# Shorter runs of empty matmuls in the opening of a fused RWKV-5 attention and squared-ReLU FFN kernel

## The chip, the cores and the metric

The kernel runs on one core of a Trainium2 chip. The metric is the device time of one execution in microseconds; lower is better. Engines are named as in the profile: PE is TensorE, PEld its weight loads, DVE VectorE, ACT ScalarE, POOL GpSimd, SP SyncE; SPq and POOLq are the parts of SP and POOL that issue transfers.

## The reference

The attention runs over r, k and v of shape (4, 8, 768, 48): batch, heads, tokens, head width. For each batch and head it keeps a 48 x 48 state:

```
y[t]  = r[t] @ (state + outer(u * k[t], v[t]))
state = w[:, None] * state + outer(k[t], v[t])
```

The eight heads of a token are put side by side (8 x 48 = 384), which gives x with 3072 rows, and the FFN follows:

```
h = maximum(x @ w_in, 0)          # 384 x 2048
out = (h * h) @ w_out             # 2048 x 384
```

All inputs and the output are float32.

## The kernel before, in words

The 768 tokens of each batch are cut into six chunks of 128, so there are 24 units (chunk, batch); units 0 to 3 are the first chunk of the four batches. A unit goes through these steps, and each step is one short function of the class `Do`:

- `ld` brings r, k or v of the unit to the chip (SP issues it, line 388). `kh` and `rh` scale k and r by powers of w into the bf16 tile rk (lines 428, 434).
- `T` transposes rk on PE with eight matmuls against an identity (line 464), and `Tc` copies the result from its PSUM bank to the tile rkT on ACT (line 286). Later units use a transposing transfer, `XB`, instead.
- `A` multiplies the transposed k and r (line 494), `Bm` masks the product on DVE (line 507), `Y` multiplies it with v in bf16 (`vb`) and, from unit 4 on, adds the state's part (lines 531, 527). `P0`, `P1`, `du` and `dv` make the part with u; `xs` adds it to Y on DVE (line 560).
- `U`, `S0`, `ts` and `S` carry the state to the next chunk.
- `X` transposes the unit's result on PE (line 578), and `xTc` copies it to the FFN's input xT; later units use a transfer, `xX`.

The FFN works on groups of units: the first two groups are one unit each, the other eleven are two. `F1.g.s` makes one slice of h for group g (line 594), `re` and `sq` take the maximum with zero and the square on ACT or DVE (lines 602, 604, 609, 613), `F2.i.f.n` adds n of the 16 parts of the second product for unit i (line 622), `os` and `out` bring the result to memory.

The weights w_in come as slices of 384 KB into staging tiles `st` (`lW.0.s`, issued by SP, line 399) and are cast to bf16 by `cW.0.s` on ACT, DVE or POOL (lines 286, 288). For groups of one unit F1.g.s uses the cast slices 2s and 2s + 1: F1.0.2 needs cW.0.4 and cW.0.5, F1.1.3 needs cW.0.6 and cW.0.7. Slice 2 and all of w_out come by a casting transfer that POOL issues (`W`, line 418).

The order of all steps is written out by hand in the string `ORDER` (line 24). A step is written as name, unit or group, then a colon, the engine (A, D, G for POOL, P, S for SP) and the buffer slots that it uses. The loop at line 676 issues the steps in that order, so each engine runs its own steps strictly in the order of the string and waits only for data and for slots. PE's first steps are

```
Z.83.6  T.3  T.0  Z.31.6  A.0  A.3  T.1  Z.22.0  A.1  T.2  U.0  Y.0  Z.15.7  X.0  A.2  Z.8.0 ...
```

`Z.n.b` is a run of empty matmuls: identity times identity into the PSUM bank b, which nobody reads before it is overwritten. n counts units of 128 columns; n // 4 of the matmuls are wide (128 x 512, line 648), and the n % 4 that remain are narrow (128 x 128, line 650). They wait for nothing but the identity. All of them stand in the opening, before the last PE step of F1.0.2.

Of the kernel before, what the change touches and what calls it, by code (L numbers as in the profile page):

```python
# [22 lines left out]
POOLS = dict(ldr=7, ldk=7, ldv=7, st=6, rk=7, P0=5, dv=5, vb=8, rkT=7, Bm=6, xs=5, hr=6, hq=30, os=4, ts=2, xT1=2, xT2=3)  # L23
ORDER = """
ld.r.0:S/0 ld.k.3:S/0 w:A shw:D u:S shu:D tab:A logw:A WkQ:A/0 kh.3:D/0 ld.k.0:S/1 P0.0:G/0 WtQ:A/1 rh.0:D/1 ld.r.3:S/1
rh.3:D/0 Z.83.6:P T.3:P/2 Tc.3:A/0 kh.0:D/1 ld.r.1:S/2 rh.1:D/2 P0.3:G/1 P1.3:G ld.r.2:S/3 rh.2:D/3 du.3:D/0 ld.k.2:S/2
T.0:P/3 Tc.0:A/1 Z.31.6:P A.0:P/4/5 ld.k.1:S/3 A.3:P/6/7 kh.2:D/3 kh.1:D/2 T.1:P/2 P1.0:G du.0:D/1 Tc.1:A/2 lW.0.0:S/0
P0.1:G/2 Bm.0.0:D/0 Bm.0.1:D/1 Bm.3.1:D/2 ld.v.0:S/0 Z.22.0:P A.1:P/1/3 P1.1:G du.1:D/2 T.2:P/0 cW.0.0:A vb.0:G/0 U.0:P/2
Bm.1.0:D/3 lW.0.1:S/1 dv.0:G Y.0:P/4 xs.0:D/0 cW.0.1:A Z.15.7:P X.0:P/5 ld.v.3:S/1 vb.3:G/1 dv.3:G Bm.1.1:D/4 Bm.3.0:D/5
Tc.2:A/3 A.2:P/7/1 Bm.2.1:D/0 ld.v.1:S/2 dv.1:G ld.v.2:S/3 vb.2:G/2 Z.8.0:P Y.3:P/4 vb.1:A/3 xs.3:D/1 Y.1:P/3 U.3:P/6  # L30
xs.1:D/2 xTc.0:A/0 F1.0.0:P/0 X.3:P/1 xTc.3:A/0 lW.0.4:S/2 cW.0.4:A WtS:A U.2:P/4 X.1:P/3 Bm.2.0:D/1 lW.0.5:S/3 Y.2:P/5
P0.2:G/3 xTc.1:D/1 F1.1.0:P/1 re.1.0:A/0 lW.0.6:S/4 cW.0.6:A P1.2:G re.0.0:D/1 du.2:D/3 dv.2:D cW.0.5:G Z.7.3:P F1.0.2:P/7
W.0.2:G F1.1.2:P/3 re.1.2:A/2 lW.0.7:S/5 cW.0.7:D F1.1.3:P/1 re.1.3:A/3 xs.2:D/3 X.2:P/0 xTc.2:D/0 F1.0.3:P/3 re.0.3:A/4
re.0.2:D/5 sq.0.2:D2/0 sq.1.3:D2/1 lW.0.3:S/0 cW.0.3:G W.1.0:G W.1.1:G ld.r.4:S/4 rh.4:D/4 WkS:A wc:S F1.2.4:P/1 WLcol:A
WLm:G F1.2.1:P/5 re.2.1:D/5 sq.2.1:D2/2 re.2.4:A/3 sq.2.4:A0/3 sq.1.0:A0/4 F1.2.3:P/0 re.2.3:A/5 ld.k.4:S/4 P0.4:D/4 kh.4:G/4
# [78 lines left out]
    kh=["rk{0}"], rh=["rk{0}"], T=["bT{0}"], Tc=["rkT{0}"], XB=["rkT{0}"], A=["bA{0}0", "bA{0}1"], Bm=["Bm{0}{1}"], Y=["bY{0}"],  # L114
    xs=["xs{0}"], U=["bU{0}"], ts=["ts{0}"], X=["bX{0}"], xTc=["xT{0}"], xX=["xT{0}"], F1=["bH{0},{1}"], re=["hr{0},{1}"],
# [608 lines left out]
```

## Time and profile before

| | |
|---|---|
| three timed runs | 176.63, 174.48, 176.38 us (median 176.38) |
| the profiled execution | 175.66 us, span 173.5 us |
| PE busy | 163.4 us, 94% of the span, 1718 matmuls |
| DVE, ACT, POOL busy | 138.6, 105.8, 100.3 us |
| transfers | 29.13 MB; q1 (SP's and ACT's) 73.8% of 16 engines' span, q0 (POOL's) 6.2% |
| wide empty matmuls (line 648) | 38, busy 10.9 us, first start at 2.7 us, last at 20.1 us |
| narrow empty matmuls (line 650) | 14 |

The profile describes one execution. All its times count from the start of the span, so 8.80 is 8.80 us after it. Matmuls are pipelined: the starts of the weight loads show the pace of PE better than the lengths of the matmuls. An entry such as `[0.40 <-DMA ldk<-in_k_dram]` says that the engine was idle for 0.40 us just before, until that transfer landed. The chain that ended last follows the end of the execution back, at each step to what released it.

### The profile page before, as it was taken

The page shows a single profiled execution, that of the slowest core. Times are in us where ns is not written, and L with a number is a line of the kernel's source. Part 1 is how long each engine was busy: PE and PEld are TensorE (multiplying, and loading weights), DVE is VectorE, ACT ScalarE, POOL GpSimd, SP SyncE. Part 2 cuts the span into 40 slices and gives each one's busy share as a digit, 9 for nine tenths or more (in the row PEclk, how much of TensorE's full clock was granted, in tenths as well). Part 3 has the DMA queues.
Part 4 walks back from the last instruction along what each step waited for, and adds up shares of the span by engine and source line. Part 5 has one row for each costly group of instructions (what it writes and reads, how often), then busy time and mean ns, then how long its engine had stood idle before and what let it go on. Part 6 is the DMA issues. An engine that isn't in the chain of part 4 may idle for free.

```text
span 173.5 us, 4403 instructions
## 1 busy us (share of the span) xinstructions
PE 163.4 (94%) x1718; PEld 121.8 (70%) x1718; DVE 138.6 (80%) x257; ACT 105.8 (61%) x189; POOL 100.3 (58%) x118
## 2 busy tenths in 40 slices
PE   3999989989999999999997999899999999998992
PEld 1476869756877777877775786686786886875871
DVE  5789879979997798989798999799979776970430
ACT  2359669764787395777564894475693482451940
POOL 5678957525199999877959763788635805100000
PEclk9999999999999999999999999999999999999999
DMA  4999999999998989999799893994991451321202
GB/s 96 229 278 225 326 217 178 213 215 191 214 196 163 225 195 210 177 194 279 148 223 204 167 227 97 191 213 84 193 229 44 106 128 37 126 68 29 91 3 88
DMA packets 105588, 29.13 MB, mean 168 GB/s; under 512 B 98008, under 2 KB 105568, under 8 KB 105568
## 3 DMA queue, kind: packets, MB, share of 16 engines
q1 hardware_dynamic: 103672, 26.95, 73.8%
q0 software_dynamic: 1744, 1.77, 6.2%
q8 instruction: 13, 0.21, 0.5%
q10 hardware_dynamic: 152, 0.14, 0.2%
q14 instruction: 7, 0.06, 0.1%
HBM read 20.46 MB, written 4.72 MB: 145 GB/s over the span
## 4 chain that ended last, share of the span: by engine, by line
PE 57%; DMA 13%; DVE 8%; SPq 8%; POOL 6%; issue 3%; ACT 2%; DVEq 0%; POOLq 0%
PE bank L594 25%; PE bank L622 23%; SPq L388 6%; DMA xT<-xs 5%; DMA st<-in_moe_w_in_dram 4%; DMA rkT<-rk 3%; DVE hq L613 2%; PE bank L494 2%; SPq L399 2%; DMA ldv<-in_v_dram 2%; PE bank L531 2%; PE bank L636 2%; PE bank L527 1%; ACT hr L602 1%; ACT hq L609 1%
## 5 line engine op out<-in xcount | busy, mean ns | idle before, releaser
L594 PE MATMUL bank<-xT,W 128*128 128x256 bf16 (+1 forms) x624 | 71.0, 264 | 2.0 <-DMA xT<-xs 1.3
L622 PE MATMUL bank<-W,hq 128*128 128x384 bf16 x368 | 68.4, 326 | 0.2 <-ACT hq L609 0.2
L594 PEld LDWEIGHTS <-W 128*128 128x128 bf16 x624 | 55.7, 98 | 11.4 <-DMA xT<-xs 1.0
L602 ACT ACTIVATE hr<-bank 128x512 bf16<-128x512 f32 x65 | 38.1, 592 | 24.6 <-PE bank L594 22.5
L609 ACT ACTIVATE hq<-hr 128x512 bf16<-128x512 bf16 x71 | 43.3, 627 | 13.5 <-DVE hr L604 12.3
L622 PEld LDWEIGHTS <-hq 128*128 128x128 bf16 x368 | 34.2, 98 | 18.8 <-ACT hq L609 0.6
L507 DVE TENSOR_TENSOR Bm<-bank,maskJT 128x512 bf16<-128x512 f32 x48 | 31.3, 681 | 3.7 <-PE bank L494 3.7
L604 DVE TENSOR_SCALAR hr<-bank 128x512 bf16<-128x512 f32 x31 | 21.1, 685 | 10.4 <-PE bank L594 10.1
L449 POOL TENSOR_TENSOR dv<-ldv,du 128x384 f32<-128x384 f32 x18 | 16.4, 913 | 14.2 <-DVE du L444 9.4
L441 POOL TENSOR_TENSOR P<-P,ub 128x384 f32<-128x384 f32 x18 | 18.9, 1055 | 7.0 <-DVE P L437 6.4
L437 POOL TENSOR_TENSOR P<-ldr,ldk 128x384 f32<-128x384 f32 x16 | 16.6, 1042 | 3.4 <-DMA ldk<-in_k_dram 3.4
L560 DVE TENSOR_TENSOR xs<-bank,dv 128x384 bf16<-128x384 f32 x24 | 13.1, 553 | 4.5 <-PE bank L531 2.7
L573 POOL TENSOR_TENSOR S0W<-ts,WLm 128x384 bf16<-128x384 f32 x11 | 11.1, 1017 | 9.5 <-DVE ts L570 9.3
L428 POOL TENSOR_TENSOR rk<-ldk,Wkhat 128x384 bf16<-128x384 f32 x14 | 15.3, 1097 | 2.2 <-DMA ldk<-in_k_dram 2.1
L286 ACT COPY os<-bank 128x384 f32<-128x384 f32 (+1 forms) x17 | 7.9, 462 | 13.4 <-PE bank L622 11.5
L444 DVE TENSOR_REDUCE du<-P 128x8 f32<-128x384 f32 x24 | 13.0, 546 | 0.9 <-POOL P L441 0.7
L648 PE MATMUL bank<-identity 128*128 128x512 bf16 x38 | 10.9, 431 | 2.7 <-POOL identity masks.py:199 2.7
L613 DVE TENSOR_TENSOR hq<-hr 128x512 bf16<-128x512 bf16 x25 | 11.9, 488 | 0.3
L434 POOL TENSOR_TENSOR rk<-ldr,Wt 128x384 bf16<-128x384 f32 x9 | 9.9, 1102 | 2.1 <-DMA ldr<-in_r_dram 2.1
L531 PE MATMUL bank<-vb,Bm 128*128 128x48 bf16 x192 | 10.9, 183 | 0.2 <-DVE Bm L507 0.2
L286 ACT COPY rkT<-bank 128x1024 bf16<-128x1024 bf16 x7 | 7.0, 1014 | 6.5 <-PE bank L464 6.5
L531 PEld LDWEIGHTS <-Bm 128*128 128x128 bf16 x192 | 9.3, 96 | 1.3 <-DVE Bm L507 0.7
(67 smaller groups left out, 160.2 us busy)
## 6 DMA issues: line engine op xcount, KB each, us to landing
ldr<-in_r_dram SPq DMA_DIRECT2D x24, 192.0 KB, 3.7
ldk<-in_k_dram SPq DMA_DIRECT2D x24, 192.0 KB, 3.8
ldv<-in_v_dram SPq DMA_DIRECT2D x24, 192.0 KB, 4.4
out_dram<-os SPq DMA_DIRECT2D x23, 192.0 KB, 3.0
st<-in_moe_w_in_dram SPq DMA_DIRECT2D x7, 384.0 KB, 5.3
W<-in_moe_w_out_dram POOLq DMA_DIRECT2D x4, 384.0 KB, 7.0
rkT<-rk SPq DMA_TRANSPOSE x17, 3.7
W<-in_moe_w_in_dram POOLq DMA_DIRECT2D x1, 192.0 KB, 5.0
```

The costliest lines, as they stand in the source:

```text
L428: e.tensor_mul(scaled("k", i), loaded("k", i), early("WkQ") if i < EARLY else Wkhat)
L437: e.tensor_mul(P0b[slot[f"P{i}"]], loaded("r", i), loaded("k", i))
L441: e.tensor_mul(t, t, ub)
L449: e.tensor_mul(dvb[slot[f"dv{i}"]], loaded("v", i), t)
L507: e.tensor_mul(o, a, mask_b)
L531: e.matmul(y[:, hc, D * h : D * (h + 1)], m[h][:, hc, :], vb[:, 2 * hc + h, :], start=(i < B), stop=True, skip_group_check=True,)
L594: e.matmul(hp[:, fi, :], W1[f // 2][:, c, 128 * (f % 2) : 128 * (f % 2 + 1)], xt[:, c, :], start=(c == 0), stop=(c == CCH - 1), skip_group ...
L602: e.activation(hr, hp, AF.Relu)
L604: e.tensor_scalar_max(hr, hp, 0.0)
L609: e.activation(hq, hr, AF.Square)
L613: e.tensor_mul(hq, hr, hr)
L622: e.matmul(bank(f"bO{i}")[:, 0:d_model], hqb[slot[f"hq{g},{f // m}"]][:, at : at + L], W2[f // 4][:, f % 4, :], start=(summed[i] == 1), st ...
```

## The change

Four of the six runs of empty matmuls get a smaller count. Nothing else differs: the steps, their order and their slots are those of before.

```diff
-rh.3:D/0 Z.83.6:P T.3:P/2 Tc.3:A/0 ...
+rh.3:D/0 Z.48.6:P T.3:P/2 Tc.3:A/0 ...
-T.0:P/3 Tc.0:A/1 Z.31.6:P A.0:P/4/5 ...
+T.0:P/3 Tc.0:A/1 Z.30.6:P A.0:P/4/5 ...
-Bm.1.0:D/3 lW.0.1:S/1 dv.0:G Y.0:P/4 xs.0:D/0 cW.0.1:A Z.15.7:P X.0:P/5 ...
+Bm.1.0:D/3 lW.0.1:S/1 dv.0:G Y.0:P/4 xs.0:D/0 cW.0.1:A Z.14.7:P X.0:P/5 ...
-P0.2:G/3 xTc.1:D/1 F1.1.0:P/1 ... cW.0.5:G Z.7.3:P F1.0.2:P/7
+P0.2:G/3 xTc.1:D/1 F1.1.0:P/1 ... cW.0.5:G Z.6.3:P F1.0.2:P/7
```

| run | before: wide + narrow | after: wide + narrow |
|---|---|---|
| first, ahead of T.3 | 20 + 3 | 12 + 0 |
| second, ahead of A.0 | 7 + 3 | 7 + 2 |
| third, Z.22, ahead of A.1 | 5 + 2 | 5 + 2 |
| fourth, ahead of X.0 | 3 + 3 | 3 + 2 |
| fifth, Z.8, ahead of Y.3 | 2 + 0 | 2 + 0 |
| sixth, ahead of F1.0.2 | 1 + 3 | 1 + 2 |

More of the change, by code (lines that the diff above doesn't have):

```diff
@@ L25 @@
 ld.r.0:S/0 ld.k.3:S/0 w:A shw:D u:S shu:D tab:A logw:A WkQ:A/0 kh.3:D/0 ld.k.0:S/1 P0.0:G/0 WtQ:A/1 rh.0:D/1 ld.r.3:S/1
-rh.3:D/0 Z.83.6:P T.3:P/2 Tc.3:A/0 kh.0:D/1 ld.r.1:S/2 rh.1:D/2 P0.3:G/1 P1.3:G ld.r.2:S/3 rh.2:D/3 du.3:D/0 ld.k.2:S/2
-T.0:P/3 Tc.0:A/1 Z.31.6:P A.0:P/4/5 ld.k.1:S/3 A.3:P/6/7 kh.2:D/3 kh.1:D/2 T.1:P/2 P1.0:G du.0:D/1 Tc.1:A/2 lW.0.0:S/0
+rh.3:D/0 Z.48.6:P T.3:P/2 Tc.3:A/0 kh.0:D/1 ld.r.1:S/2 rh.1:D/2 P0.3:G/1 P1.3:G ld.r.2:S/3 rh.2:D/3 du.3:D/0 ld.k.2:S/2
+T.0:P/3 Tc.0:A/1 Z.30.6:P A.0:P/4/5 ld.k.1:S/3 A.3:P/6/7 kh.2:D/3 kh.1:D/2 T.1:P/2 P1.0:G du.0:D/1 Tc.1:A/2 lW.0.0:S/0
 P0.1:G/2 Bm.0.0:D/0 Bm.0.1:D/1 Bm.3.1:D/2 ld.v.0:S/0 Z.22.0:P A.1:P/1/3 P1.1:G du.1:D/2 T.2:P/0 cW.0.0:A vb.0:G/0 U.0:P/2
-Bm.1.0:D/3 lW.0.1:S/1 dv.0:G Y.0:P/4 xs.0:D/0 cW.0.1:A Z.15.7:P X.0:P/5 ld.v.3:S/1 vb.3:G/1 dv.3:G Bm.1.1:D/4 Bm.3.0:D/5
+Bm.1.0:D/3 lW.0.1:S/1 dv.0:G Y.0:P/4 xs.0:D/0 cW.0.1:A Z.14.7:P X.0:P/5 ld.v.3:S/1 vb.3:G/1 dv.3:G Bm.1.1:D/4 Bm.3.0:D/5
 Tc.2:A/3 A.2:P/7/1 Bm.2.1:D/0 ld.v.1:S/2 dv.1:G ld.v.2:S/3 vb.2:G/2 Z.8.0:P Y.3:P/4 vb.1:A/3 xs.3:D/1 Y.1:P/3 U.3:P/6
 xs.1:D/2 xTc.0:A/0 F1.0.0:P/0 X.3:P/1 xTc.3:A/0 lW.0.4:S/2 cW.0.4:A WtS:A U.2:P/4 X.1:P/3 Bm.2.0:D/1 lW.0.5:S/3 Y.2:P/5
-P0.2:G/3 xTc.1:D/1 F1.1.0:P/1 re.1.0:A/0 lW.0.6:S/4 cW.0.6:A P1.2:G re.0.0:D/1 du.2:D/3 dv.2:D cW.0.5:G Z.7.3:P F1.0.2:P/7
+P0.2:G/3 xTc.1:D/1 F1.1.0:P/1 re.1.0:A/0 lW.0.6:S/4 cW.0.6:A P1.2:G re.0.0:D/1 du.2:D/3 dv.2:D cW.0.5:G Z.6.3:P F1.0.2:P/7
 W.0.2:G F1.1.2:P/3 re.1.2:A/2 lW.0.7:S/5 cW.0.7:D F1.1.3:P/1 re.1.3:A/3 xs.2:D/3 X.2:P/0 xTc.2:D/0 F1.0.3:P/3 re.0.3:A/4
```

## The prediction

> **What bounds the kernel now.** I read four views: the page, to see which stage is limited by what; the chain that ended last, for what sets the end of the opening; the order of time on PE and its weight loads, for the pace of the empty matmuls; and the same on DVE, ACT and POOL, for what each step of the opening waits for. The page first (the row is the busy share of the DMA engines in slices of 4.34 us, in tenths).
>
> ```profile
> span 173.5 us, 4403 instructions
> ...
> DMA  4999999999998989999799893994991451321202
> ```
>
> The DMA engines are full from the second slice to the twelfth, so through the whole opening (to about 24 us). The chain in order of time, where PE takes it over:
>
> ```profile
> 15.70 6.61 DMA st<-in_moe_w_in_dram
> ...
> 22.33 0.96 DVE W L288
> ...
> 23.34 0.51 PE bank L594 x6
> ```
>
> This is the view that decides. Before these rows the chain is SP issuing transfers one behind the other from 2.7 us on; then comes the flight of one slice of w_in (6.61 us), its cast on DVE (cW.0.7), and the six matmuls of F1.1.3 that use it. No empty matmul and no transpose of PE is in it. So what matters is whether an earlier PE moves these links.
>
> **The first run of empty matmuls.** PE's weight loads in order of time (start, length, line, instructions, in brackets the wait before):
>
> ```profile
> 2.71 0.13 PEld L648 LDWEIGHTS <-identity 128*128 128x128 bf16 x2 [2.71 <-POOL identity masks.py:199]
> ...
> 5.67 0.15 PEld L648 LDWEIGHTS <-identity 128*128 128x128 bf16 x1 [0.28 <-issue]
> 6.10 2.26 PEld L648 LDWEIGHTS <-identity 128*128 128x128 bf16 x11 [0.28 <-issue]
> 8.48 0.37 PEld L650 LDWEIGHTS <-identity 128*128 128x128 bf16 x3
> 8.80 0.94 PEld L464 LDWEIGHTS <-rk 128*128 128x128 bf16 x16
> ...
> 11.52 0.45 PEld L494 LDWEIGHTS <-rkT 48*128 48x128 bf16 x16
> 12.07 0.45 PEld L464 LDWEIGHTS <-rk 128*128 128x128 bf16 x8
> ```
>
> Z.83 is 20 wide matmuls (L648) and 3 narrow ones (L650). Up to 6.10 us the loads are 0.43 us apart (5.67 to 6.10), from there 0.21 us (11 in 2.26 us): PE goes to twice its rate 3.39 us after its first matmul. Z.48 is 12 wide ones and no narrow one. The part up to 6.10 us is the same in both, so the 8 wide ones that go are fast ones: 8 x 0.206 = 1.64 us. The 3 narrow ones are 8.80 - 8.48 = 0.32 us. Together 1.96 us: the run would be out of T.3's way at 8.80 - 1.96 = 6.84 us. What T.3 then waits for is on DVE:
>
> ```profile
> 6.02 1.21 DVE L434 TENSOR_TENSOR rk<-ldr,bank 128x384 bf16<-128x384 f32 x2
> 7.15 0.55 DVE L428 TENSOR_TENSOR rk<-ldk,bank 128x384 bf16<-128x384 f32 x1
> ```
>
> rh.3 is the second of the pair at 6.02, done at 7.23; so T.3 starts at about 7.28 instead of 8.80: **1.52 us earlier**, and 0.44 us of what was removed turns into waiting. T.0 needs kh.0, done at 7.15 + 0.55 = 7.70 us, about its turn. The two copies on ACT that follow (Tc.3, Tc.0) had waited for exactly this:
>
> ```profile
> 9.51 1.93 ACT L286 COPY rkT<-bank 128x1024 bf16<-128x1024 bf16 x2 [3.52 <-PE bank L464]
> ```
>
> They start 0.71 us behind T.3's first load, so at 7.99, and end at 9.92. On PE, Z.31 took from the end of the transposes' loads (9.74) to A.0 (11.52), 1.78 us; Z.30 is one narrow one shorter (0.11 us) and ends at 8.22 + 1.67 = 9.9 too. A.0 comes at 10.0, still 1.5 us early.
>
> **Where the 1.5 us goes.** Each next step has a second input that does not move.
>
> ```profile
> 10.49 0.56 DVE L428 TENSOR_TENSOR rk<-ldk,bank 128x384 bf16<-128x384 f32 x1 [0.40 <-DMA ldk<-in_k_dram]
> 10.97 0.55 DVE L444 TENSOR_REDUCE du<-P 128x8 f32<-128x384 f32 x1
> 11.96 1.89 DVE L507 TENSOR_TENSOR Bm<-bank,maskJT 128x512 bf16<-128x512 f32 x3 [0.44 <-PE bank L494]
> ```
> ```profile
> 15.25 0.56 DVE L560 TENSOR_TENSOR xs<-bank,dv 128x384 bf16<-128x384 f32 x1 [0.30 <-PE bank L531]
> ```
>
> - T.1 needs kh.1, the DVE step at 10.49 that had waited for its transfer and ends at 11.05. T.1's loads came at 12.07, so it gains 1.0 us, not 1.5.
> - Bm.0.0 waited only 0.44 us for A; the du before it ends at 11.52 whatever PE does. So DVE gains 0.44 us here and at most 0.30 us more at xs.0: some 0.7 us.
> - The three other runs (Z.30, Z.14, Z.6) lose one narrow matmul each, 3 x 0.11 = 0.3 us. They stand where PE was going to wait for ACT or DVE, so I cost them at nothing; were that cover gone, they would be a gain of 0.3 us.
>
> PE then reaches F1.0.0 some 0.7 us early. Next come steps that wait for no PE result at all:
>
> ```profile
> 15.04 0.50 POOL L288 CAST vb<-ldv 128x384 bf16<-128x384 f32 x1 [0.78 <-DMA ldv<-in_v_dram]
> ...
> 18.61 1.00 POOL L441 TENSOR_TENSOR P<-P,ub 128x384 f32<-128x384 f32 x1
> 19.76 0.89 POOL L288 CAST W<-st 128x768 bf16<-128x768 f32 x1
> 20.60 0.93 POOL L418 DMA_DIRECT2D W<-in_moe_w_in_dram  x1
> 23.59 0.82 POOL L288 CAST W<-st 128x768 bf16<-128x768 f32 x1 [2.06 <-DMA st<-in_moe_w_in_dram]
> ```
> ```profile
> 20.55 2.10 PE L594 MATMUL bank<-xT,W 128*128 128x128 bf16 x30
> 23.34 0.51 PE L594 MATMUL bank<-xT,W 128*128 128x128 bf16 x6 [0.69 <-DVE W L288]
> ```
> ```profile
> 22.33 0.95 DVE L288 CAST W<-st 128x768 bf16<-128x768 f32 x1 [1.25 <-DMA st<-in_moe_w_in_dram]
> ```
> ```profile
> 21.20 0.89 ACT L286 CAST W<-st 128x768 bf16<-128x768 f32 x1 [0.23 <-DMA st<-in_moe_w_in_dram]
> ```
>
> POOL runs from 15.04 to 20.65 without a wait, behind a transfer; the cast at 19.76 is cW.0.5, the weights of F1.0.2's second half. F1.0.2 began at 20.55, so that half can gain 0.1 or 0.2 us, no more. Then F1.1.3 needs cW.0.6 (ACT, which waited 0.23 us for a transfer) and cW.0.7 (DVE, which waited 1.25 us for one and ends at 23.28). A DVE that is earlier only waits longer there, PE's own wait of 0.69 us grows, and POOL waits 2.06 us for such a slice at 23.59. So between 20.6 and 23.6 us **all four engines meet transfers**, and the head start is used up: the gain at F1.1.3 is 0.
>
> Would those transfers come earlier? SP's own waits up to 24 us (in total, times, longest):
>
> ```profile
> SPq L368 <- DVE du L444: 2.5, 1, 2.5
> ...
> SPq L399 <- ACT xT L286: 0.2, 1, 0.2
> ```
>
> Only the second can follow PE (that ACT copy reads a PE result): 0.2 us for the last slice, which feeds the POOL cast at 23.59 and not the chain. The du of the first needs the product that POOL ends at 19.61, and POOL's transfer at 20.60 stands behind cW.0.5: both fixed. The sum is 1.5 us at T.3, 1.0 at T.1, 0.7 at xs.0, 0 at F1.1.3. Against this execution's own time of 175.66 us (span 173.5 and 2.2 around it) I forecast **175.6 us**. The shown runs are 176.63, 174.48 and 176.38, median 176.38, so that lies inside their spread; about 2% (3.5 us) is what a measurement of this kernel can tell from no change.
>
> [...] Does less empty work lose the fast rate again? PE's longest later wait, and what follows it:
>
> ```profile
> 92.67 0.40 PE L494 MATMUL bank<-rkT 48*128 48x128 bf16 x8 [1.05 <-DMA rkT<-rk]
> 93.00 0.83 PE L594 MATMUL bank<-xT,W 128*128 128x256 bf16 x6
> 93.66 0.81 PE L622 MATMUL bank<-W,hq 128*128 128x384 bf16 x4
> ```
>
> After 1.05 us without work, six matmuls of 256 columns start within 0.66 us, 0.11 each: half of the 0.206 for 512 columns, so the fast rate holds. The gaps that the change opens by the sum above are 0.44 us before T.3 and some 0.6 us before T.1, both shorter. The risk is rather the time at which the fast rate sets in. The trace has one such start, 3.39 us after the first matmul, and both kernels are alike up to it. [...]
>
> **The rivals.**
> - *Slower: the fast rate comes late.* At 0.43 us each the 12 wide ones last to 2.71 + 5.16 = 7.87 us, T.3 and T.0 at half rate (2 x 0.94 us) to 9.8, and Z.30's seven wide ones (3.0 us) and two narrow ones to 13.0: A.0 is 1.5 us late, with PE's slack before F1.1.3 (0.69 us) and DVE's (1.25 us) to swallow most of it. If half rate lasts another 3.4 us, to 16.4 us, 1.7 us more is lost: 3.2 less 0.7 is 2.5 us, **178.2 us**. It decides from a start of the fast rate later than about 13 us; each 3.4 us beyond adds 1.7, so the next step gives 179.9. For it: only one start is seen. Against: in this trace it lies before the point where the kernels differ.
> - *Faster: the head start reaches the end.* If the slices land earlier after all, the 1.52 us goes through: **174.1 us**. About the same comes out if in timed runs the fast rate begins later than here by less than the rival above needs: with 16 of its 20 wide ones at 0.43 us the long run would hold T.3 to 10.4 us or more, the short one to 7.9. For it: two of the three runs are 2 us above the third. Against: the waits for transfers on all four engines.
> - *The removal does nothing even at T.3*, if rk.3 comes later by the loads' own scatter: 175.7, and not told from the forecast by its time.
>
> **How the numbers follow.** The forecast, the third rival with it, 0.56; the late rate 0.20, of which 0.12 beyond 2%; the head start 0.18, of which 0.03 beyond 2% with the runs' scatter on top; something unseen 0.06, half to each side. The range reaches 0.5 us below the head start's 174.1 for the scatter, and 0.8 above 178.2: 173.6 to 179.0, with just under 2 in 10 outside, mostly above. Faster by 2% (under 172.9) 0.06, slower (over 179.9) 0.15, within 0.79.
>
> **What would show it.** In the profile after: the wide matmuls again 0.43 us apart up to about 6.1; T.3's loads at 7.3 behind a wait for DVE; A.0 near 10.0; DVE's wait before cW.0.7 about 2 us instead of 1.25; F1.1.3's second half still at 23.3 with a longer wait before it; the chain again over SP and that slice. I am wrong if the loads stay 0.43 apart up to T.3 or behind it, if the slice lands at another time than 22.3, or if the two traces part by over 1 us only behind 24 us.

## The result, and the profile after

Twenty runs of each kernel: after 174.16 us median (172.69 to 176.29), before 175.62 us (173.63 to 177.70). The ratio is **0.9935, 95% interval 0.9906 to 0.9964**: some 1.1 us or 0.65% faster. The ratio takes only the executions of each kernel within 1.5% of its fastest, so it is nearer to 1 than the ratio of the two medians (0.992). The result is inside the range of the prediction and within its 2%, but it is clear of zero, and the forecast was no gain.

The profiled execution of after has a span of 172.0 us against 173.5. Its weight loads on PE in order of time (columns as before):

```profile
6.52 0.34 PEld L648 LDWEIGHTS <-identity 128*128 128x128 bf16 x2 [0.28 <-issue]
6.98 0.65 PEld L464 LDWEIGHTS <-rk 128*128 128x128 bf16 x8
7.84 0.45 PEld L464 LDWEIGHTS <-rk 128*128 128x128 bf16 x8 [0.21 <-DVE rk L428]
...
10.01 0.45 PEld L494 LDWEIGHTS <-rkT 48*128 48x128 bf16 x16
10.93 0.45 PEld L464 LDWEIGHTS <-rk 128*128 128x128 bf16 x8 [0.47 <-DVE rk L428]
```

The head start is there: T.3 begins at about 7.0 instead of 8.80, A.0 at 10.01 instead of 11.52, T.1 at 10.93 instead of 12.07. DVE and PE of after at the end of the opening:

```profile
11.26 1.88 DVE L507 TENSOR_TENSOR Bm<-bank,maskJT 128x512 bf16<-128x512 f32 x3
```
```profile
23.06 0.95 DVE L288 CAST W<-st 128x768 bf16<-128x768 f32 x1 [1.71 <-DMA st<-in_moe_w_in_dram]
```
```profile
22.84 0.51 PE L594 MATMUL bank<-xT,W 128*128 128x128 bf16 x6 [0.68 <-ACT W L286]
24.07 0.51 PE L594 MATMUL bank<-xT,W 128*128 128x128 bf16 x6 [0.72 <-DVE W L288]
```

And there it is gone. Bm.0.0 is 0.7 us early, but the second half of F1.1.3 starts at 24.07 us, which is 0.73 us *later* than before, because in this execution the slice landed that much later. At T.4 (34.01 us before) after is still 0.7 us behind, at T.5 (36.57 us), where before waits 0.59 us for DVE, 0.1 us. What is different stands much further back. PE's waits behind 90 us, in total, times and longest, first before, then after:

```profile
PE bank L594 <- DMA xT<-xs: 1.3, 2, 0.6
PE bank L494 <- DMA rkT<-rk: 1.1, 1, 1.1
PE bank L622 <- ACT hq L609: 0.2, 1, 0.2
```
```profile
PE bank L494 <- DMA rkT<-rk: 0.9, 1, 0.9
```

Before waits 1.3 us for transposing transfers to xT, after not at all. With the PE matmuls of both traces put side by side, after goes from 0.5 us behind at 90 us to 1.5 us ahead at the end: 0.2 us at the rkT wait (92.67 us of before), 0.8 at each of the xT waits (109.08 and 159.67) and 0.3 at the wait for hq (119). No step of the change lies within 70 us of any of them.

### The profile page after: what moved, and what is told of

The parts are those of the page before. It is cut to its first block, busy times and chain, and to the rows that moved or that the text cites. A ratio compares the mean times of both kernels' runs of the same rounds, so it can differ in the third digit from the quotient of the medians.

```text
span 172.0 us, 4375 instructions
## 1 busy us (share of the span) xinstructions
PE 161.9 (94%) x1704; PEld 120.9 (70%) x1704; DVE 139.2 (81%) x257; ACT 106.0 (62%) x189; POOL 100.7 (59%) x118
## 4 chain that ended last, share of the span: by engine, by line
PE 68%; DMA 8%; SPq 8%; POOL 5%; DVE 4%; ACT 3%; issue 2%; DVEq 0%; POOLq 0%
PE bank L594 29%; PE bank L622 28%; SPq L388 5%; DMA st<-in_moe_w_in_dram 4%; PE bank L494 3%; DMA rkT<-rk 3%; SPq L399 2%; PE bank L531 2%; PE bank L527 2%; PE bank L636 2%; ACT hq L609 1%; DMA ldk<-in_k_dram 1%; POOL rk L434 1%; PE bank L552 1%; POOL S0W L573 1%
## 5 line engine op out<-in xcount | busy, mean ns | idle before, releaser
L648 PE MATMUL bank<-identity 128*128 128x512 bf16 x30 | 9.4, 455 | 2.7 <-POOL identity masks.py:199 2.7
```

## The experiments

At first two theories: **absorbed** (the opening gives nothing, the rest is how late transfers happen to fall) and **carried** (part of T.3's head start reaches the end). The first four runs ask whether the result repeats, and which part of the change makes it.

The kernel before once more:

> The kernel before, unchanged, for a second profile and for the scatter of the comparison. Theory 'absorbed' (the head start is used up at the weight slices; the 1.1 us come later, from transfers that happen to land earlier or later): ratio 1.000 within 0.4%, and the waits of PE for transposing transfers behind 90 us (2.3 us in all in the first profile: 1.1, 0.6 and 0.6) differ from the first profile's by 0.5 us or more in sum or in place. Theory 'carried' (part of the head start at T.3 reaches the end): ratio 1.000 too, but these waits come again within 0.2 us in the same places.

Measured: 0.9983 (0.9954 to 1.0012). Its profiled execution is 4 us longer than the first, so only the places of its waits are used: they are again rkT at 95.66 us and xT at 113.48 and 163.87.

The kernel after once more:

> The kernel after, unchanged. Both theories: ratio near 0.9935, between 0.990 and 0.997. 'Absorbed': F1.1.3's second half starts within 0.8 us of 23.3 us, not earlier by 1 us, and the waits of PE behind 90 us differ from the first profile of after (0.9 us, one wait). 'Carried': these waits are again 0.9 us, one wait, and so about 1.4 us shorter than before's.

Measured: 0.9923 (0.9883 to 0.9962), so the gain repeats. F1.1.3's second half starts at 24.7 us, later than 'absorbed' allowed. Behind 90 us PE waits 2.6 us for rkT and again not once for xT. Neither theory had said that one kind of wait would come and go with the kernel.

Only the first run shortened:

```diff
-Z.83.6:P
+Z.48.6:P
```

> Only the first run is shortened (48 instead of 83), the other three stay. Both theories: T.3 some 1.5 us earlier than in the kernel before, A.0 near 10.1. If the gain hangs on the first run: ratio 0.994, as the whole change. If it hangs on the three narrow matmuls: 1.000.

Measured: 0.9874 (0.9826 to 0.9921, six runs). Against the first profile of before T.3 is 1.3 us earlier, A.0 only 0.8. Only the three narrow matmuls taken away:

```diff
-Z.31.6:P ... Z.15.7:P ... Z.7.3:P
+Z.30.6:P ... Z.14.7:P ... Z.6.3:P
```

> Only the three other runs lose one narrow matmul each, the first keeps 83. If the gain hangs on the first run: ratio 1.000 within 0.3%. If it hangs on the three: 0.994. By my sum at most 0.3 us, so 0.998 or more.

Measured: 0.9997 (0.9946 to 1.0048). The gain hangs on the first run.

**The opening alone, and the first run made longer or taken out.** The first pair is cut off behind Tc.4:

```diff
 ... ld.k.7:S/6 T.4:P/6 du.4:D/4 Tc.4:A/4
-sq.2.5:A0/13 sq.2.3:D2/14 ...   (all later steps)
+(384 columns of rkT4 copied and stored)
```

> The kernel before, cut off behind Tc.4 (some 37 us into the profile), with one small result stored at the end; the rest of the computation is left out. With e2 it times the opening alone, in many executions. Both theories: about 37 + 4 us of span, 43 us in all.

> The kernel after, cut off at the same place; the rest is left out. 'Absorbed': median within 0.3 us of e1's. 'Carried': 0.8 to 1.5 us below e1's, as the 1.1 us of the whole kernel, because in some timed executions the fast rate of PE begins later than in the first profile, the long run of before then holds T.3 back by more than the slices hide.

Measured: 42.40 us median (41.83 to 43.76) and 42.76 us (41.66 to 43.45), six runs each. The 0.8 to 1.5 us that "carried" expected don't show; a few tenths of a us either way can't be told with runs that lie up to 1.9 us apart.

The first run of before made longer:

```diff
-Z.83.6:P
+Z.120.6:P
```

> The kernel before with a first run of 120 (30 wide matmuls instead of 20 + 3 narrow): T.3 1.7 us later than before, at about 10.5 us. 'Absorbed': F1.1.3 has 0.7 us of slack, then at most 1 us is lost, most of it hidden by other waits: ratio 1.000 to 1.004. 'Carried': the loss is near the whole delay, 1.2 to 1.9 us: ratio 1.007 to 1.011.

Measured: **0.9942** (0.9906 to 0.9977). A first run that is *longer* by 1.7 us gains as much as the shorter one, with T.3 in its profile 3.0 us later than in the first profile of before. That was expected by no theory: it ends "carried", and "absorbed" too, which had 1.000 or more.

The first run taken out of after:

```diff
-Z.48.6:P
```

> The kernel after without the first run. T.3 starts at about 7.3 us as in after, but at half rate. If the fast rate needs 3.4 us of work like that of the run, it sets in at 11 us or later: T.3 and T.0 take 1.9 us, Z.30 3.2 us, A.0 comes at 12.4 or later. 'Absorbed': about 1 us later than before at A.0, mostly hidden: ratio 1.000 to 1.006 against before. The late-rate rival: half rate up to 16 us or more, 1.010 or more.

Measured: 0.989 (0.9823 to 0.9956, six runs). No loss from a late rate either: the rows stand in the last section.

**A new theory: fetch.** 83 has a ratio of 1, and 48, 120 and none lie below it. What differs, apart from the time at T.3, is the number of PE's instructions. The profile lists a DMA queue of its own for instructions:

```profile
q8 instruction: 13, 0.21, 0.5%
```

That is 13 packets of 16 KB, and the kernel before has 2 x 1718 = 3436 weight loads and matmuls: one packet for about 264 of them. (The expectations count two more for every kernel, 3438 for 3436; the differences between kernels are the same.) In the traces a packet starts on average each time PE has gone through some 250 of them (208 to 302 from one to the next in before, 188 to 300 in after; one stood at 2219 to 2239 loads and matmuls in all eight profiles so far, whatever came before), which is why q8 is taken for PE's own queue, and each packet takes 0.9 to 1.7 us. If the packets keep to the count, 28 loads and matmuls less in the opening move later fetches by 28 places in the program. That is an inference: by the count, the n-th packets of the two traces stand 4 to 40 places apart. The transfers and packets in a window around the xT transfer of 105.5 us, in before, and around the same transfer in after (queue: packets, MB, share of 16 engines; then the transfer, with the us to landing):

```profile
q8 instruction: 1, 0.02, 2.0%
xT<-xs SPq DMA_TRANSPOSE x1, 3.5
```
```profile
q1 hardware_dynamic: 448, 0.12, 24.4%
xT<-xs SPq DMA_TRANSPOSE x1, 2.3
```

In before an instruction packet falls into the flight (it starts 1.0 us behind the issue) and the transfer takes 3.49 us; in after the window holds none and it takes 2.28. The next runs cross the two: T.3 early or late, and the count as before or as after.

T.3 early, count as before. In after, four wide matmuls are cut into 16 narrow ones, which took as long here (the first wide one behind them starts at 4.38 us, as the fifth wide one of after):

```diff
-Z.48.6:P ... Z.30.6:P ... Z.14.7:P
+N.16.6:P Z.32.6:P ... Z.31.6:P ... Z.15.7:P     (N.n.b: n narrow ones)
```

> New theory 'fetch': PE's instructions are brought in by transfers of 16 KB (queue q8, 13 of them, one per about 250 PE instructions), and one that falls into the flight of a transposing transfer makes that transfer 1.2 to 1.8 us longer; the change takes 28 PE instructions out of the opening and so moves every later fetch against the program. This kernel has the early T.3 of after, but PE's instruction count of before (3438 weight loads and matmuls): of the 12 wide matmuls of the first run, four are cut into 16 narrow ones, which take as long at half rate, and two runs get their narrow matmul back. 'Fetch': the gain is gone, 1.000 within 0.4% against before; the transposing transfer for xT that is issued at about 106 us takes 3.4 us or more. 'Head start': 0.992, as after, since T.3 is as early; that transfer's length is open.

Measured: **1.0005** (0.9960 to 1.0051). The first load of its T.3, and the PE rows at the two places where before had waited for xT:

```profile
7.37 0.15 PEld L464 LDWEIGHTS <-rk 128*128 128x128 bf16 x1 [0.28 <-DVE rk L434]
```
```profile
110.24 1.48 PE L594 MATMUL bank<-xT,W 128*128 128x256 bf16 x12 [0.49 <-DVE rk L434]
...
160.57 5.40 PE L594 MATMUL bank<-xT,W 128*128 128x256 bf16 x48 [0.63 <-DMA xT<-xs]
```

T.3 is as early as in the repeated after (7.38), and both waits are back. The first is put down to DVE here, but it ends as the xT transfer lands (issued at 106.80, 3.40 us to landing).

T.3 late, count as after. From before, the runs ahead of A.1 and X.0 are taken out:

```diff
-Z.31.6:P ... Z.22.0:P ... Z.15.7:P
+Z.30.6:P
```

> The late T.3 of before (first run 83), but PE's instruction count of after (3410): the runs ahead of A.1 and X.0 are gone and the second has one narrow matmul less. 'Fetch': 0.992 within 0.4%, as after; the xT transfer issued at about 106 us takes 2.3 us. 'Head start': 1.000.

Measured: **0.9918** (0.9872 to 0.9963). T.3 and the waits behind 90 us:

```profile
9.59 0.94 PEld L464 LDWEIGHTS <-rk 128*128 128x128 bf16 x16
```
```profile
PE bank L494 <- DMA rkT<-rk: 1.4, 2, 1.1
```

T.3 is later here than in the profile before, the whole gain is there, and no wait for xT is left. The two runs that are gone don't make the opening earlier either: F1.1.3's second half starts at 24.18 us and T.5 at 36.81, against 23.34 and 36.57 in the first profile of before.

T.3 early, count as in the kernel with the longer run. In after, seven of the 12 wide matmuls are cut into 28 narrow ones:

```diff
-Z.48.6:P
+N.28.6:P Z.20.6:P
```

> The early T.3 of after with 42 PE instructions more than after (3452, as in the kernel with the longer first run): seven of its 12 wide first matmuls are cut into 28 narrow ones. 'Fetch': as the kernel with the longer run, 0.990 to 0.994, and lower still, near 0.988, if the 1.5 us that T.3 gains against that kernel reach the end. 'Head start': 0.992 as after.

Measured: 0.9921 (0.9881 to 0.9960). The first part came, the second (0.988) didn't: T.3's head start is worth nothing that shows here either.

Before without any empty matmul:

```diff
-Z.83.6:P ... Z.31.6:P ... Z.22.0:P ... Z.15.7:P ... Z.8.0:P ... Z.7.3:P
```

> The kernel before without any of the six runs of empty matmuls: PE's count falls by 104 to 3334, and each later fetch of PE's instructions moves 104 weight loads and matmuls later in the program. By the 11 profiles so far the fetches then fall between most of the transposing transfers: the xT transfers issued at about 93, 105 and 155 us should take 2.6, 2.3 and 3.0 us; about 4 of the 27 transposing transfers should still meet a fetch, against 8 or 9 before. 'Fetch': ratio 0.983 to 0.992 against before, as the kernel without the first run (0.989) or a little below it. Late-rate rival: PE stays at half rate through much of the opening, F1.1.3's second half starts later than 26 us and the ratio is 1.000 or more.

Measured: 1.0003 (0.9957 to 1.0049). Two of the three transfers are as forecast (2.28 and 3.00 us; the first took 3.01, not 2.6). The ratio isn't, and neither is the number of transfers that meet a fetch: 10 of 27, not about 4. Its PE, in order of time:

```profile
19.22 1.48 PE L594 MATMUL bank<-xT,W 128*128 128x128 bf16 x12
...
21.82 3.17 PE L594 MATMUL bank<-xT,W 128*128 128x128 bf16 x48 [0.25 <-DVE xT L288]
```

F1.0.0 at 19.22 takes 1.48 us for 12 matmuls, where it took 0.83 us in before: here PE is at half rate until some 21 us. F1.1.3's second half starts at 24.5 us, not later than 26, so the late-rate rival is only half met. The profiled execution is the fastest of the twelve (175.42 us, median 177.39); how long half rate lasts in the others isn't known, and what it costs was not separated.

All twelve profiles of whole kernels in one table, with the start of the fetch counted from the issue of the transfer ("-": none within the flight or 1.2 us before it). Starts and landings are read from the traces' records.

| kernel | loads and matmuls on PE | xT of 105 us: fetch, us to landing | xT of 155 us: fetch, us to landing | ratio |
|---|---|---|---|---|
| before | 3436 | +1.0, 3.49 | +1.8, 4.52 | 1 |
| before once more | 3436 | +1.2, 4.12 | +2.2, 4.52 | 0.9983 |
| T.3 early, old count | 3436 | +1.0, 3.40 | +1.9, 4.50 | 1.0005 |
| three narrow ones only | 3430 | +1.8, 4.11 | -, 2.99 | 0.9997 |
| first run only | 3414 | +2.3 (as it lands), 2.28 | -, 2.99 | 0.9874 |
| after | 3408 | -, 2.28 | -, 3.00 | 0.9935 |
| after once more | 3408 | +2.3 (as it lands), 2.29 | -, 2.99 | 0.9923 |
| T.3 late, new count | 3408 | -, 2.28 | -, 3.00 | 0.9918 |
| first run gone | 3384 | -, 2.28 | -, 2.98 | 0.9890 |
| longer first run | 3450 | -0.9, 2.57 | +1.2, 3.60 | 0.9942 |
| T.3 early, longer count | 3450 | +0.5, 2.95 | +2.2, 4.53 | 0.9921 |
| no empty matmuls | 3332 | -, 2.28 | -, 3.00 | 1.0003 |

The two columns of xT don't give the ratio by themselves: both kernels with 3450 meet a fetch at 155 us and still lie near 0.993, and the one without empty matmuls meets neither. There are 25 other transposing transfers, and each count trades some meetings for others. Of all 27, 9 or 10 meet a fetch (one that starts between 1.2 us before the issue and 0.1 us before the landing) in the four profiles with a ratio within 0.2% of 1: before, before once more, T.3 early with the old count, and no empty matmuls. In the others 6 to 8 do, at ratios of 0.987 to 0.994; only the kernel with three narrow ones less (7, at 0.9997) falls out. This was counted behind the runs, so it is a fit and not a test, and how the meetings add up to each ratio stays open. What the crossed pair shows is that the count of PE's instructions moves the time (0.9918 against 1.0005, with 1.1 us between the means of the executions that these ratios take) and that an earlier T.3 brings no gain without it.

## Why the prediction was right or wrong

- **The first run's end, T.3, A.0, T.1: right.** T.3 at 7.28 was forecast and 7.0 came (the transposes begin with k's half of rk.3, and I had counted from r's), A.0 at 10.0 and 10.01, T.1 at 11.1 and 10.93.
- **DVE's share: mis-sized.** 0.44 us at Bm.0.0 was a term; it measured 0.70 (11.26 against 11.96), since the k transfer before it landed 0.2 us sooner. At xs.0 the gain was 1.0 us (14.23 against 15.25) where 0.7 was forecast, but PE reached F1.0.0 only 0.4 us early (17.29 against 17.66), not 0.7.
- **All four engines meet transfers, gain 0 at F1.1.3: right.** The slice at 23.06 us ended the head start, and DVE's wait grew from 1.25 to 1.71 us (about 2 forecast). The slice itself came 0.7 us later than the 22.3 us that the prediction had named, one of its signs of being wrong; F1.1.3's second half moved with it, and not with PE. That nothing of the head start reaches the end agrees with the cut-off pair (42.40 and 42.76 us) and with T.3 early and the old count (1.0005).
- **The three narrow matmuls at nothing: right.** Without them the ratio was 0.9997 (0.9946 to 1.0048).
- **"The sum is ... 0 at F1.1.3", so 175.6: this step failed.** It ended the sum at 24 us, as if a change that leaves no time there leaves none anywhere. The term that was missing, minus 1.1 us, goes with the count of PE's instructions, and it comes 70 us and more behind the last changed step. The traces point to the place of the instruction fetches as the way it acts; that their sum gives the 1.1 us isn't shown. The page's row of q8 got no price in the prediction. The prediction named this outcome as one that would prove it wrong (the traces part only behind 24 us), and it did.
- **The rival "faster" had the time, 174.1, and the wrong mechanism.** That the result lies within the range is partly luck, since this rival's head start had set the lower end. With T.3 early and the old count the ratio is 1.0005, with T.3 late and the new count 0.9918.
- **"Does nothing even at T.3": not met.** T.3 came 1.8 us earlier (6.98 against 8.80).
- **The rival "slower": not met by this change.** Half rate lasts longer than to 6.10 us in some executions: in the repeated after the loads stay 0.43 us apart up to T.3 (7.38 us, below), another sign that the prediction had named, and the ratio was 0.9923 all the same. And even without the first run PE reached the full rate at about 10.4 us, before its bound of 13 us. That half rate lasts another 3.4 us, as its sum has it, no profile of a whole kernel with a first run shows: the loads change pace at 6.10 us in before, 6.95 in before once more, 7.38 with three narrow ones less and 7.81 in the repeated after. A start of the full rate behind 13 us is seen only with all six runs gone (some 21 us).

## What to carry to other kernels

In this kernel, which waits for transposing transfers, the number of instructions ahead of them on PE's long instruction stream was itself worth about 1% (0.9918 against 1.0005). So before crediting a small gain to the edited step, pad the instruction count back and see whether the gain stays. And a gain from a changed opening should be looked for in a cut-off opening first; here two short kernels showed none of the expected size in six runs each.

## What the runs showed of the hardware that was not expected

**Instruction fetches and transposing transfers.** In twelve profiles there are 27 transposing transfers each. The 80 in whose flight a PE fetch starts take 4.37 us on average, the 226 with none in the flight or in the 1.2 us before it 3.25 us (the other 18 have one that starts in those 1.2 us). Compared transfer by transfer, for the 21 that have both cases, the difference is 0.86 us on average, 1.3 us for the xT transfer of 155 us (5 with, 7 without), 1.0 us for that of 105 us (7 and 4) and 1.4 us for that of 93 us (7 and 5). That is about the length of a fetch (0.9 to 1.7 us). The traces record sixteen landings for each transfer, and these tell more. In the xT transfer of 155 us in before, fifteen came by 2.98 us and the last at 4.52; in 10 of all 324 transfers the last came over 0.3 us behind the fifteenth, and in each of the 10 an instruction packet had started in the flight, 0.5 to 1.3 us ahead of the fifteenth (PE's in 7, only an 8 KB packet of queue q14 in 3). So in these 10 a single sixteenth that comes late goes with a fetch that started late in the flight. In the transfer of 105 us in before, where the fetch starts 1.0 us behind the issue, all sixteen are late (the first at 3.25 us, 2.15 in after). Which DMA engine carried the packet isn't recorded, so that the two share one is an inference and not shown. The 8 KB packets don't make the difference at the transfer of 155 us: one starts 1.3 us behind its issue in all twelve profiles.

**When PE reaches full rate.** Loads of the repeated after and of the kernel without its first run:

```profile
7.38 0.15 PEld L464 LDWEIGHTS <-rk 128*128 128x128 bf16 x1 [0.27 <-issue]
7.81 1.08 PEld L464 LDWEIGHTS <-rk 128*128 128x128 bf16 x15 [0.28 <-issue]
```
```profile
6.10 0.34 PEld L464 LDWEIGHTS <-rk 128*128 128x128 bf16 x4 [6.10 <-DVE rk L428]
...
10.01 0.15 PEld L648 LDWEIGHTS <-identity 128*128 128x128 bf16 x1 [0.27 <-issue]
10.44 0.34 PEld L648 LDWEIGHTS <-identity 128*128 128x128 bf16 x2 [0.28 <-issue]
```

With the same first matmul at 2.7 us, full rate came at 6.1 us in the first profile of before and at 7.8 us in this one. What sets it is not shown. Without the first run the change of pace is at 10.4 us, 4.3 us behind the first transposes; without any empty matmul it is at some 21 us, and PE stood idle for about 1 us several times on the way, as in these rows of that kernel:

```profile
10.37 1.04 PE L494 MATMUL bank<-rkT 48*128 48x128 bf16 x16 [1.13 <-ACT rkT L286]
...
14.14 0.61 PE L494 MATMUL bank<-rkT 48*128 48x128 bf16 x8 [1.10 <-ACT rkT L286]
```
